# A two-layer Fourier and sliding-window attention kernel: zeros ahead of the first rows, and the last round's norm steps spread

## The chip, the cores and the metric

One core of a Trainium2 chip runs the whole program in one launch. The metric is device time in microseconds: 2034.66 is the median of three runs (2031.99, 2034.66, 2038.42). Five engines each work through a queue of their own: PE (TensorE, matrix products), DVE (VectorE), ACT (ScalarE), POOL (GpSimd) and SP (SyncE, which here issues nearly every DMA). In the profile PEld is the loading of weights into TensorE.

## The reference

The input x has 2048 rows and 640 columns. Two layers of different kinds follow each other, twice:

```python
x = x + _A_ref(_layernorm(x), dft_seq_re, dft_seq_im, dft_hid_re, dft_hid_im)   # spectral
x = x + _B_ref(_layernorm(x), wqkv, wo)                                         # attention
x = x + _A_ref(...)
x = x + _B_ref(...)

# A: a = x @ hid_re.T ; b = x @ hid_im.T ; y = seq_re @ a - seq_im @ b
# B: qkv = x @ wqkv, 32 heads of 20; row q sees keys q-255..q; softmax; @ wo
```

All data is float32. The layer norm subtracts a row's mean and divides by sqrt(variance + 1e-5).

## The kernel before, in words

**Precision.** TensorE multiplies float16. Each float32 operand is therefore kept as two float16 parts, a high part (a rounded copy) and a low part (what is left), and each product is three matrix products: high by high, high by low, low by high. Making the parts is much of what ACT (high parts), DVE (low parts) and POOL do.

**A spectral layer.** `spectral` first multiplies the normed rows with the hidden-size matrices (`z_stage`) and then with the sequence matrix, in four rounds r of eight steps j. For each step a 1 MB piece of the matrix is loaded by SP (`load_c`, tile `cq`), POOL makes four sums of its quarters (`take_c`, L549 to L552, tile `cs`), and seven high parts (ACT, L557) and seven low parts (DVE, L560) of quarters and sums become `cc`. The step's seven products use them, each of twelve 128x320 matmuls (`main_a`, `main_b`, `main_c`, banks x, y, z). Results are added into `res` by DVE (`add`, L583), ACT (L602) and POOL (L603, L613, L624).

After each product stands one `tick()`. A tick issues one of the splits of a coming piece, and one step of each generator in the list `side`. So work beside the products is placed by how many `yield`s stand between its instructions: a yield is one product, about 1.6 us of TensorE.

In the last round (r=3) the finished rows x2 are stored, and attention's input is begun there. `finish(0, ..)` and `finish(1, ..)`, chained in `side` from the end of step j=0 on, load back two pages of 128 rows each and run `norm_steps` for the pair: statistics (L138, L141), the reciprocal root of the variance by three Newton steps on single columns (L147 to L155), then ACT's normed page `lny` (L163). `pace` is the number of ticks for each step of it. Then `transposed` (L449) turns a page: TensorE transposes it in float32 against an identity `idf`, three 128-column pieces and then two, into one of two PSUM banks of tag f (`pf`), ACT makes the high part (L455), DVE the low part (L456, which frees the bank). As soon as `finish(0, ..)` is through, `ahead(proj)` issues ten query and key projections of 15 matmuls 128x256 each. Their evacuation is ACT `qf` (L386), POOL's cast (L387) and subtraction (L388), and a store to `qkd`; from there SP loads the stacks `ks` for the scores, behind tiles of ones.

**An attention layer.** `attention` interleaves scores, softmax and values, in a fixed order of TensorE, with units of other work from a list `fill`: value projections (the first of which stands right behind the last product of the spectral layer), query and key projections, output tiles ("out"), and, in layer 0 alone, the next layer's first hidden products ("next", from `Hidden.stage` with once=True). `next_unit` takes the unit due first out of those that are ready, in wide slots and narrow ones. L1272 is ACT's exponential, whose table ACT loads at L1411 before the first one.

**What sets the order.** The kernel writes the order by hand: each engine issues in the order in which the program states, with some instructions held behind others. At the start of layer 0 the order of loads on SP's queue, and DVE's splits of the first matrix pieces (L560) and of the first rows (L456), come from the lines of `spectral` around `constants()`, `load_c(0)` and `take_c(0)`.

Of the kernel before, what the change touches and what calls it, by code (L numbers as in the profile page):

```python
# [13 lines left out]
I32 = mybir.dt.int32  # L14
AF = mybir.ActivationFunctionType
# [58 lines left out]
def body(ctx: ExitStack, tc: tile.TileContext, x_in, cmat, whid, wqkv, wo, out):  # L74
# [56 lines left out]
    def norm_steps(xs, ys, act=False):  # L131

        n = len(xs)
        mv = keep.tile([P, n, 2], F32, tag=f"lnmv{n}", name="lnmv", bufs=2)
        for k, x in enumerate(xs):
            st = keep.tile([P, 2, 6], F32, tag="lnst", name="lnst", bufs=2)
            for h in range(2):
                nc.vector.bn_stats(st[:, h], x[:, h * 320:(h + 1) * 320])  # L138
                if h == 0:
                    yield  # L140
            nc.vector.bn_aggr(mv[:, k], st.rearrange("p a b -> p (a b)"))  # L141
            yield
        t = keep.tile([P, 3, n], F32, tag=f"lnt{n}", name="lnt", bufs=2)
        ts = nc.vector.tensor_scalar
        for k in range(n):
            h, g, u = (t[:, m, k:k + 1] for m in range(3))
            ts(h, mv[:, k, 1:2], 1e-5, -0.5 * X_UP ** -2, op0=OP.add, op1=OP.mult)  # L147
            ts(g.bitcast(I32), h.bitcast(I32), -0.5, ROOT, op0=OP.mult, op1=OP.add)
            for m in range(3):
                ts(u, g, g, h, op0=OP.mult, op1=OP.mult)  # L150
                normed[0] = ts(g, u, 1.5, g, op0=OP.add, op1=OP.mult).ins  # L151
                if m == 0:
                    yield
            if act:
                normed[0] = ts(u, mv[:, k, 0:1], g, -1.0, op0=OP.mult, op1=OP.mult).ins  # L155
            yield
        for _ in range(2 if act else 0):
            yield
        for k, x in enumerate(xs):
            g, u = t[:, 1, k:k + 1], t[:, 2, k:k + 1]  # L160
            y = keep.tile([P, D], F32, tag="lny", name="lny", bufs=2)
            if act:
                nc.scalar.activation(y, x, AF.Identity, bias=u, scale=g)  # L163
            else:
                normed[0] = ts(y, x, mv[:, k, 0:1], g, op0=OP.subtract, op1=OP.mult).ins
            ys.append(y)
            yield
# [55 lines left out]
    class Hidden:  # L223
# [29 lines left out]
        def stage(self, s, pool, new=new_f, once=False):  # L253
# [21 lines left out]
                z = z[:, :HD]  # L275

            def parts(m, f):
                nc.scalar.activation(zc[:, m, 0], f, AF.Copy)  # L278
                nc.gpsimd.tensor_tensor(zc[:, m, 1], f, zc[:, m, 0], op=OP.subtract)  # L279

            def scaled(o):
# [118 lines left out]
    def spectral(layer, res_src, hidden, first):  # L400
        with ExitStack() as st:
# [226 lines left out]
            def main_c(r, j):  # L628
                res, cc, y, zb = state.pop((r, j))
                x0, x1 = res  # L630
                z = product(r, zb, cc, 6, False, True)
                add(x0[:, hi], z, x0[:, hi])
                tick()
                z = product(r, y, cc, 5, False, True)
                add(x1[:, lo], z, x1[:, lo])
                last = r == NR - 1
                for k in range(2):
                    load((x2_d if last else acc_d)[2 * j + k], res[k])
                if last and j == 0:
                    side.append(chain(finish(0, 1), finish(1, 1)))  # L640
                tick()

            def ahead(proj):
                while finished[0] < 2:
                    yield 1
                yield 1
                for w in (1, 0):
                    for ct in range(ND):
                        for _ in proj.qk(0, w, ct):
                            pass  # L650
                        yield 1
# [98 lines left out]
                return [max(NJ * r + STAGES[r][k] - 3, k) for r in range(NR - 1)]  # L750

            if first:
                constants()
                x = [load_x(s) for s in range(2)]
                f = [load_w(n) for n in range(NXIN - 2)]
                norm_x(0, x[:1], nc.vector)
                for n in range(10):
                    split_w(n, f[n])
                    if n == 1:
                        turn_x(0)  # L760
                        turned_x(0)
                        norm_x(1, x[1:], nc.gpsimd)
                    if n == 7:
                        x = [load_x(s) for s in range(2, 4)]
                    if n + NXIN - 2 < 10:
                        f.append(load_w(n + NXIN - 2))
            load_c(0)
            for r in range(NR):
                for k in range(RS if r == 0 else 0):
                    s = RS * r + k  # L770
# [7 lines left out]
                            turn_x(s + 1, 2)  # L778
                    elif s > 1:
                        hidden.fetch(s)  # L780
                    if r == 0 and k == 1:
                        load_c(1)
                        with behind() as order:
                            if not first:
                                order.enter_context(tc.issue_after(hidden.after))
                            take_c(0)
# [56 lines left out]
    def attention(layer, proj, dst, final):  # L843
        with ExitStack() as st:
# [261 lines left out]
            def next_unit(wide=None):  # L1106
# [3 lines left out]
                if 2 * left() >= must_to() - now[0] % (2 * NP):  # L1110
                    us = [u for u in us if must(u)] or us
                us = [u for u in us if u.wide == wide] or us
                u = min(us, key=lambda u: u.due)
                fill.remove(u)
                return u
# [396 lines left out]
```

## Time and profile before

| | us |
|---|---|
| median of three runs | 2034.66 |
| the profiled execution | 2034.73 |
| its span, first to last instruction | 2033.0 |
| PE busy | 1978.8 (97%) |
| DVE busy | 1556.2 (77%) |
| POOL busy | 1438.2 (71%) |
| ACT busy | 1098.1 (54%) |
| granted TensorE clock, mean | 0.999 |

A row of the timeline holds start, duration, engine, line of the code, operation, out<-in with partitions, shape and type, and the count of instructions. In brackets stands how long the engine was idle ahead of it, and what ended that. A row of windows holds the window, its length, the busy time of PE, PEld, DVE, ACT and POOL (with the count of instructions), the granted TensorE clock, the busy share of the DMA engines, and GB/s. A row of groups holds the busy time and the mean in ns of one instruction, and then the idle time before them with what ended it. Layer 0's last round ends near 548 us and layer 1's near 1554; attention 0 ends near 1010.

### The profile page before, as it was taken

How to read it: one execution, taken by the hardware profiler on the slowest of the kernel's cores; microseconds unless marked ns; L12 is line 12 of the kernel's file. 1: busy time of each engine (PE TensorE's matmuls, PEld its weight loads, DVE VectorE, ACT ScalarE, POOL GpSimd, SP SyncE). 2: the span in 40 equal slices, each digit the busy share in tenths (PEclk: the TensorE clock that was granted, in tenths of full speed). 3: DMA queues.
4: the chain of work that ended last, by engine and by line, in shares of the span. 5: the costliest groups of instructions: out<-in, count | busy, mean ns of one | idle time of the engine just before them, and what ended most of it. 6: DMA issues, size and time to landing. Idle time of an engine off the chain costs nothing.

```text
span 2033.0 us, 55567 instructions
## 1 busy us (share of the span) xinstructions
PE 1978.8 (97%) x21761; PEld 1446.6 (71%) x21761; DVE 1556.2 (77%) x3281; ACT 1098.1 (54%) x1962; POOL 1438.2 (71%) x2148
## 2 busy tenths in 40 slices
PE   7999999999999999999999999999999999999998
PEld 5777777776777777777667777777677677777765
DVE  8888788767688888777648778787766788886674
ACT  5444555543257677666644444444332577766665
POOL 4667788877568788765557778777774687777754
PEclk9999999999999999999999999999999999999999
DMA  8566467566545545434545465454754455443232
GB/s 276 185 195 212 167 212 233 184 240 213 144 99 130 126 112 122 101 100 114 157 133 179 157 183 183 150 171 150 266 184 122 106 124 123 118 120 94 75 81 80
DMA packets 280507, 311.08 MB, mean 153 GB/s; under 512 B 107572, under 2 KB 214836, under 8 KB 271156
## 3 DMA queue, kind: packets, MB, share of 16 engines
q1 hardware_dynamic: 279668, 306.88, 51.3%
q8 instruction: 170, 2.79, 0.6%
q14 instruction: 93, 0.76, 0.1%
q10 hardware_dynamic: 576, 0.66, 0.1%
HBM read 201.72 MB, written 83.46 MB: 140 GB/s over the span
## 4 chain that ended last, share of the span: by engine, by line
PE 72%; DVE 12%; issue 4%; ACT 3%; DMA 2%; POOL 2%; SPq 0%; DVEq 0%; ACTq 0%; POOLq 0%
PE pf L125 33%; PE y L125 12%; PE x L125 12%; PE z L125 8%; PE sk L125 5%; DVE cc L560 3%; PE sq L125 3%; DVE sq L1216 2%; ACT ptq L1272 2%; DVE m L1218 2%; DMA res<-accd 1%; DVE lnst L138 1%; DVE lnt L150 1%; DVE res L583 1%; DVE lnt L151 1%
## 5 line engine op out<-in xcount | busy, mean ns | idle before, releaser
L125 PEld LDWEIGHTS <-cc 128*128 128x128 f16 x5376 | 525.9, 98 | 211.2 <-issue 11.1
L1272 ACT ACTIVATE ptq<-sk,shift,alpha 128x768 f32<-128x768 f32 (+2 forms) x512 | 472.7, 945 | 134.2 <-PE sk L125 70.5
L125 PEld LDWEIGHTS <-big 128*128 128x128 f16 x4320 | 411.9, 98 | 132.9 <-issue 27.0
L1218 DVE TENSOR_REDUCE m<-sq 128x2 f32<-128x512 f32 (+1 forms) x512 | 345.2, 674 | 18.9
L557 ACT ACTIVATE cc<-cs 128x512 f16<-128x512 f32 x256 | 153.1, 623 | 273.0 <-POOL cs L550 151.5
L125 PE MATMUL pf<-early,big 128*128 128x256 f16 x2400 | 288.1, 273 | 4.2 <-ACT qf L386 3.8
L1216 DVE COPY_PREDICATED sq<-mask,sk 128x256 f32<-128x256 int32 x512 | 216.4, 423 | 69.3 <-PE sq L125 65.9
L125 PE MATMUL y<-zc,cc 128*128 128x320 f16 x1728 | 262.1, 299 | 3.2 <-DVE pf L583 3.2
L1276 POOL TENSOR_SCALAR_AFFINE_SELECT ptq<-ptq 128x512 f32<-128x512 f32 x224 | 142.7, 637 | 170.6 <-ACT ptq L1272 169.2
L560 DVE SCALAR_TENSOR_TENSOR cc<-cs,cc 128x512 f16<-128x512 f32 x256 | 246.4, 971 | 6.0 <-ACT cc L557 6.0
L560 DVE SCALAR_TENSOR_TENSOR cc<-cq,cc 128x512 f16<-128x512 f32 x192 | 204.4, 1066 | 0.1
L125 PE MATMUL pf<-ptq,v 128*32 128x128 f32 (+1 forms) x3840 | 183.9, 330 | 4.8 <-DVE x L990 3.7
L125 PE MATMUL z<-zc,cc 128*128 128x320 f16 x1152 | 177.7, 299 | 2.9 <-DVE res L583 1.9
L1278 POOL TENSOR_SCALAR_AFFINE_SELECT ptq<-ptq 128x512 f32<-128x512 f32 x256 | 164.6, 643 | 22.4 <-ACT ptq L1272 22.3
L125 PE MATMUL x<-zc,cc 128*128 128x320 f16 x1152 | 177.7, 299 | 0.0
L549 POOL TENSOR_TENSOR cs<-cq 128x512 f32<-128x512 f32 x64 | 85.3, 1333 | 87.8 <-DVE cc L560 64.8
L386 ACT ACTIVATE qf<-pf 128x256 f32<-128x256 f32 x160 | 60.9, 382 | 156.4 <-PE pf L125 108.4
L125 PEld LDWEIGHTS pf<-ptq,v 128*32 128x32 f32 x3840 | 110.9, 110 | 47.5 <-DVE x L990 5.7
L125 PE MATMUL pf<-big,early 128*128 128x320 f16 x960 | 141.4, 300 | 0.0
L125 PEld LDWEIGHTS <-qs 62*128 62x128 f16 x2688 | 90.2, 94 | 59.2 <-issue 56.0
L279 POOL TENSOR_TENSOR zc<-big,zc 128x320 f16<-128x320 f32 x96 | 74.7, 792 | 73.6 <-ACT zc L278 73.6
L125 PE MATMUL pf<-bo,ot 128*128 128x320 f16 x840 | 124.6, 301 | 0.8 <-DVE x L990 0.8
(147 smaller groups left out, 3443.3 us busy)
## 6 DMA issues: line engine op xcount, KB each, us to landing
cq<-in_cmat_dram SPq DMA_DIRECT2D x64, 1024.0 KB
accd<-res SPq DMA_DIRECT2D x96, 320.0 KB
res<-accd SPq DMA_DIRECT2D x96, 320.0 KB
x<-x2d SPq DMA_DIRECT2D x64, 320.0 KB
qkd<-early SPq DMA_DIRECT2D x160, 128.0 KB
ks<-qkd SPq DMA_DIRECT2D x108, 160.0 KB
qs<-qkd SPq DMA_DIRECT2D x84, 160.0 KB
x2d<-res SPq DMA_DIRECT2D x32, 320.0 KB
```

The source lines that it names most:

```text
L125: i = getattr(nc.tensor, what)(*args, **kw)
L138: nc.vector.bn_stats(st[:, h], x[:, h * 320:(h + 1) * 320])
L279: nc.gpsimd.tensor_tensor(zc[:, m, 1], f, zc[:, m, 0], op=OP.subtract)
L386: nc.scalar.activation(f, pf[:, :QB], AF.Copy, scale=down)
L549: g.tensor_tensor(s1, a21, a22, op=OP.add)
L557: nc.scalar.activation(cc[m][:, 0], f, AF.Copy, scale=C_UP)
L560: nc.vector.scalar_tensor_tensor(cc[m][:, 1], f, C_UP, cc[m][:, 0], op0=OP.mult, op1=OP.subtract)
L1216: marks["dve"] = nc.vector.copy_predicated(near[pi][:, :, 0], mask[:, None, :].to_broadcast([P, 2, P]), farq[pi]).ins
L1218: marks["dve"] = nc.vector.tensor_reduce(TOP[n][:, pi, :, k], near[pi][:, :, :1 + (i >= 1)], axis=AX.XY, op=OP.max).ins
L1272: marks["act"] = nc.scalar.activation(o[:, pi], tps[pi][:, :, first:], AF.Sigmoid, bias=shift, scale=alpha[:, 0:1]).ins
L1276: nc.gpsimd.affine_select(out=q[:, :, a0], in_=q[:, :, a0], pattern=[[0, 4], [-1, P]], base=0, channel_multiplier=1, compare_op=OP.is_gt, ...
L1278: ins = nc.gpsimd.affine_select(out=q[:, :, a0 + 2], in_=q[:, :, a0 + 2], pattern=[[0, 4], [1, P]], base=0, channel_multiplier=-1, compare ...
```

## The change

Five things change. (1) In the first layer, ahead of everything, DVE sets a tile to zero and TensorE does 28 matmuls 128x512 on it, whose result nobody reads. The statement `load_c(0)` stands later in the first layer, at s=1, and `load_c(1)` with `take_c(0)` one s later. (2) The eight copies that make a high part in the next layer's first hidden products (`parts`, once=True) go from ACT to POOL. (3) The Newton steps of a pair of pages run on both columns at once, with one tick after each of the three. (4) `finish(0, ..)` has pace 2 in the place of 1, and `ahead` waits one tick more. (5) `next_unit` prefers, where there is a choice, "next" units in narrow slots and others in wide ones.

```diff
@@ norm_steps
-        for k in range(n):
+        if n > 1 and act:
+            h, g, u = (t[:, m] for m in range(3))
+            ts(h, mv[:, :, 1], 1e-5, -0.5 * X_UP ** -2, op0=OP.add, op1=OP.mult)
+            ts(g.bitcast(I32), h.bitcast(I32), -0.5, ROOT, op0=OP.mult, op1=OP.add)
+            for m in range(3):
+                nc.vector.tensor_tensor(u, g, g, op=OP.mult)
+                nc.vector.tensor_tensor(u, u, h, op=OP.mult)
+                normed[0] = nc.vector.scalar_tensor_tensor(g, u, 1.5, g, op0=OP.add, op1=OP.mult).ins
+                yield
+            normed[0] = nc.vector.scalar_tensor_tensor(u, mv[:, :, 0], -1.0, g, op0=OP.mult, op1=OP.mult).ins
+            yield
+        for k in range(0 if n > 1 and act else n):
@@ Hidden.stage, parts
-                nc.scalar.activation(zc[:, m, 0], f, AF.Copy)
+                if once:
+                    nc.gpsimd.tensor_copy(zc[:, m, 0], f)
+                else:
+                    nc.scalar.activation(zc[:, m, 0], f, AF.Copy)
@@ main_c
-                    side.append(chain(finish(0, 1), finish(1, 1)))
+                    side.append(chain(finish(0, 2), finish(1, 1)))
@@ ahead
-                yield 1
+                for _ in range(2):
+                    yield 1
@@ spectral
             if first:
+                nc.vector.memset(bo[0][:, 0], 0.0)
+                pt = new_f()
+                for _ in range(28):
+                    matmul(pt, bo[0][:, 0, :P], bo[0][:, 0, :512], start=True, stop=True)
                 constants()
...
-            load_c(0)
+            if not first:
+                load_c(0)
...
-                    if r == 0 and k == 1:
+                    if first and r == 0 and k == 1:
+                        load_c(0)
+                    if r == 0 and k == 1 + first:
                         load_c(1)
@@ next_unit
                 us = [u for u in us if u.wide == wide] or us
+                us = [u for u in us if (u.kind == "next") != wide] or us
```

The order in which the instructions stand moves at three places. The first is DVE near the end of the first rows' work in layer 0 (`big` is the turned rows, `cc<-cq` a low part of the first matrix piece). Before:

```order
L285 SCALAR_TENSOR_TENSOR early<-y,early 128x320
L560 SCALAR_TENSOR_TENSOR cc<-cq,cc 128x512
L456 SCALAR_TENSOR_TENSOR big<-pf,big 128x384
L285 SCALAR_TENSOR_TENSOR early<-z,early 128x320
L285 SCALAR_TENSOR_TENSOR big<-z,big 128x320
L560 SCALAR_TENSOR_TENSOR cc<-cs,cc 128x512
L456 SCALAR_TENSOR_TENSOR big<-pf,big 128x256
```

The same place of the change (L560 is now L574, L456 is L470, L285 is L299):

```order
L299 SCALAR_TENSOR_TENSOR early<-y,early 128x320
L470 SCALAR_TENSOR_TENSOR big<-pf,big 128x384
L299 SCALAR_TENSOR_TENSOR early<-z,early 128x320
L299 SCALAR_TENSOR_TENSOR big<-z,big 128x320
L470 SCALAR_TENSOR_TENSOR big<-pf,big 128x256
L574 SCALAR_TENSOR_TENSOR cc<-cq,cc 128x512 x3
```

The rows' low parts stand ahead of the piece's low parts, and no longer among them. On SP, the loads of the first piece stand at the same place as before.

The second place is the norm of a pair of pages on DVE in the last round, from the second aggregate on. Before:

```order
L141 BN_AGGR lnmv<-lnst 128x2
L148 TENSOR_SCALAR lnt<-lnt 128x1
L560 SCALAR_TENSOR_TENSOR cc<-cq,cc 128x512
L150 TENSOR_SCALAR lnt<-lnt 128x1
L147 TENSOR_SCALAR lnt<-lnmv 128x1
L583 SCALAR_TENSOR_TENSOR res<-z,res 128x320
L151 TENSOR_SCALAR lnt<-lnt 128x1
L148 TENSOR_SCALAR lnt<-lnt 128x1
L560 SCALAR_TENSOR_TENSOR cc<-cs,cc 128x512
L150 TENSOR_SCALAR lnt<-lnt 128x1 x2
L151 TENSOR_SCALAR lnt<-lnt 128x1 x2
```

The change, from the first root instruction on (L583 is now L597):

```order
L147 TENSOR_SCALAR lnt<-lnmv 128x2
L574 SCALAR_TENSOR_TENSOR cc<-cs,cc 128x512
L148 TENSOR_SCALAR lnt<-lnt 128x2
L150 TENSOR_TENSOR lnt<-lnt 128x2
L151 TENSOR_TENSOR lnt<-lnt 128x2
L152 SCALAR_TENSOR_TENSOR lnt<-lnt 128x2
L597 SCALAR_TENSOR_TENSOR res<-z,res 128x320
L574 SCALAR_TENSOR_TENSOR cc<-cs,cc 128x512
L150 TENSOR_TENSOR lnt<-lnt 128x2
```

An instruction now does both columns of the pair, and adds (L597) stand between the three Newton steps.

The third place is ACT at the end of the last round of layer 0, with what each instruction waits for (`early` is the turned pages, `lny` the normed ones, L1411 the exponential's table and its first use). Before:

```order
L455 ACTIVATE early<-pf 128x384 [waits PE_49]
L455 ACTIVATE early<-pf 128x256 [waits PE_49]
L602 ACTIVATE pf<-x 128x320 [waits PE_49,Pool_49]
L557 ACTIVATE cc<-cs 128x512
L1411 ACT_TABLE_LOAD [waits PE_49,Activation_49]
L1411 ACTIVATE first<-shift 128x1 [waits Pool_49]
L902 ACTIVATE v<-pf 128x16x20 [waits PE_49] x2
```

The change (L163 is now L174, L455 is L469, L1411 is L1434, L902 is L924):

```order
L571 ACTIVATE cc<-cs 128x512
L174 ACTIVATE lny<-x_6339,lnt 128x640 [waits DMAHW0_49,DVE_49]
L174 ACTIVATE lny<-x_6340,lnt 128x640 [waits DMAHW3_49]
L1434 ACT_TABLE_LOAD [waits PE_49,Activation_49]
L1434 ACTIVATE first<-shift 128x1 [waits Pool_49]
L469 ACTIVATE early<-pf 128x384 [waits PE_49]
L469 ACTIVATE early<-pf 128x256 [waits PE_49]
L924 ACTIVATE v<-pf 128x16x20 [waits PE_49] x2
```

The second pair's normed pages and their evacuations have moved behind all splits of the spectral layer, the evacuations behind the table load too, directly ahead of the first value projection. On TensorE the ten transposes of that pair stand there in a row:

```order
L125 MATMUL pf<-idf,lny 128x128 [waits Activation_49]
L125 MATMUL pf<-idf,lny 128x128 x4
L125 MATMUL pf<-idf,lny 128x128 [waits DVE_49]
L125 MATMUL pf<-idf,lny 128x128 x2
L125 MATMUL pf<-idf,lny 128x128 [waits DVE_49]
L125 MATMUL pf<-idf,lny 128x128
L125 LDWEIGHTS early
L125 MATMUL pf<-big,early 128x320 [waits DVE_49]
```

Before, they stand in four groups between the products of step j=7, and nothing stands between the last product and the projection.

## The prediction

> **What bounds the kernel now.** I read the page's busy shares and the chain of waits first, then the timeline at each place that the change touches, then windows and groups there.
>
> ```profile
> PE 1978.8 (97%) x21761; PEld 1446.6 (71%) x21761; DVE 1556.2 (77%) x3281; ACT 1098.1 (54%) x1962; POOL 1438.2 (71%) x2148
> ...
> PE 72%; DVE 12%; issue 4%; ACT 3%; DMA 2%; POOL 2%; SPq 0%; DVEq 0%; ACTq 0%; POOLq 0%
> ...
> 250.00:300.00 50.00, 50.00 (x372) 36.23 (x370) 40.28 (x68) 27.76 (x55) 42.26 (x35) 1.00 0.62 209
> ```
>
> TensorE is busy 1978.8 of a span of 2033.0 us, and in the middle of a spectral layer 50.00 of 50.00 at granted clock 1.00. So an edit can only win part of the 54.2 us in which TensorE stands still, or of the time at a lower clock, and it loses whatever new standstill it makes. No matmul that the result needs is removed. The profiled execution took 2034.73 us, 1.73 around its span; the median of the runs is 2034.66, so a sum made on the one holds for the other.
>
> **Start: zeros, and the order behind them.** These rows are the first work.
>
> ```profile
> 3.88 0.89 DVE L138 BATCH_NORM_STATS2 lnst<-xin 128x6 f32<-128x320 f32 x2 [3.88 <-DMA xin<-in_x_dram]
> 8.47 1.30 PE L125 MATMUL pf<-idf,lny 128*128 128x128 f32 x5 [8.47 <-DVE lny L165]
> 9.38 0.81 ACT L455 ACTIVATE big<-pf 128x384 f16<-128x384 f32 x2
> 9.93 0.72 PE L125 MATMUL y<-big 128*128 128x320 f16 x2 [0.15 <-ACT big L455]
> 10.76 0.88 DVE L456 SCALAR_TENSOR_TENSOR big<-pf,big 128x384 f16<-128x384 f32 x2
> 12.58 1.11 PE L125 MATMUL z<-big 128*128 128x320 f16 x7
> ```
>
> The memset is on DVE, idle until 3.88; it costs nothing. The first two 320-column products start .50 apart (9.93 to the next row at 10.43), so about .25 each; seven later take about .95, .135 each. Scaled to 512 columns, 28 zero products last 28 x .40 = 11.2 us if all run at the slow rate, 6.0 if all at the fast. With the slow rate for the first 3 to 4 us I estimate 7 to 8 us; starting near 1.2 us, they end at 8.1 to 9.2, beside a first need for TensorE at 8.47. ACT finishes its high parts at 10.19, DVE starts the low parts at 10.76: .57 of slack. Nor does a faster TensorE here gain: it then waits for DVE (2.13 us of work in the three between 14 and 17). I take **0**, between -0.3 and +0.75, and +3.9 if all 28 run slow (1.2 + 11.2 = 12.4 against 8.47).
>
> ```profile
> 14.00:17.00 3.00, 2.13 (x16) 1.41 (x15) 3.00 (x3) 0.91 (x2) 2.92 (x2) 1.00 0.76 213
> 31.04 1.28 DVE L560 SCALAR_TENSOR_TENSOR cc<-cq,cc 128x512 f16<-128x512 f32 x2
> 33.04 0.68 DVE L560 SCALAR_TENSOR_TENSOR cc<-cq,cc 128x512 f16<-128x512 f32 x1
> 34.25 1.40 PE L125 MATMUL x<-big 128*128 128x320 f16 x9 [1.52 <-DVE big L456]
> 41.79 0.55 DVE L456 SCALAR_TENSOR_TENSOR big<-pf,big 128x384 f16<-128x384 f32 x1
> ```
>
> In the program's order of the changed kernel, the first piece's four quarter loads stand where they stood in the SP queue, fourth behind the first rows, so that part **does not do what its words say**: nothing of the loads moves. What moves is DVE: L456 now stands ahead of three low parts of the matrix (1.28 + .68 us) instead of behind them. The 1.52 us wait at 34.25 can go; but the next L456, at 41.79, has the same DVE work ahead of it, less some .5 to 1.0 that the row order saves, so TensorE catches up with DVE there. I take **-0.8**, from -1.6 (the wait, wholly) to +0.3 (the split of a piece that comes later).
>
> **Last round of each spectral layer: norm steps spread.** Between the products of step j=6, DVE has the norm's small instructions ahead of the adds that TensorE waits for.
>
> ```profile
> 466.93 1.79 PE L125 MATMUL z<-zc,cc 128*128 128x320 f16 x12 [1.05 <-DVE res L583]
> 470.32 3.42 PE L125 MATMUL y<-zc,cc 128*128 128x320 f16 x24 [1.59 <-DVE pf L583]
> 494.39 1.80 PE L125 MATMUL pf<-early,big 128*128 128x256 f16 x15 [1.47 <-ACT qf L386]
> 1472.85 1.79 PE L125 MATMUL z<-zc,cc 128*128 128x320 f16 x12 [1.04 <-ACT cc L557]
> 1476.23 3.42 PE L125 MATMUL y<-zc,cc 128*128 128x320 f16 x24 [1.59 <-DVE pf L583]
> 1500.29 1.80 PE L125 MATMUL pf<-early,big 128*128 128x256 f16 x15 [1.46 <-ACT qf L386]
> ...
> 468.25 0.44 DVE L150 TENSOR_SCALAR lnt<-lnt 128x1 f32<-128x1 f32 x2
> 469.78 0.48 DVE L583 SCALAR_TENSOR_TENSOR pf<-y,pf 128x320 f32<-128x320 f32 x1
> ```
>
> The six waits sum to 1.05 + 1.59 + 1.47 + 1.04 + 1.59 + 1.46 = 8.2 us. The roots of two pages were 18 instructions a pair; ten of them fill the block from 468.25 to the add at 469.78, .15 us each. Together they are 12, and no more than five stand between two adds. An instruction on 128x2 is not in the trace; it lies between the .15 of 128x1 and the .48 of 128x320, and I take .2. So a pair costs 2.4 us instead of 2.7, but in portions of 1 us and less with an add between them. Low parts of the matrix that DVE owes at that time (.68 each alone, as at 33.04) are still there, so I leave .8 of each layer's wait standing, and .3 for a query/key evacuation: 8.2 - 2 x 1.1, **-6.0**, from -8.2 to -3.
>
> **What is pushed back.** The same spread delays all that follows. Before, the ten transposes of pages 2 and 3 stand between j=7's products, their evacuations hidden under 1.6 us products:
>
> ```profile
> 530.30 0.49 PE L125 MATMUL pf<-idf,lny 128*128 128x128 f32 x3
> 530.63 1.79 PE L125 MATMUL y<-zc,cc 128*128 128x320 f16 x12
> 532.26 0.38 PE L125 MATMUL pf<-idf,lny 128*128 128x128 f32 x2
> 535.22 0.48 ACT L455 ACTIVATE early<-pf 128x384 f16<-128x384 f32 x1
> 535.74 0.56 DVE L456 SCALAR_TENSOR_TENSOR early<-pf,early 128x384 f16<-128x384 f32 x1 [0.85 <-ACT early L455]
> 536.48 0.38 ACT L455 ACTIVATE early<-pf 128x256 f16<-128x256 f32 x1 [0.78 <-PE pf L125]
> ...
> 547.69 2.20 PE L125 MATMUL pf<-big,early 128*128 128x320 f16 x15
> 547.96 1.28 ACT L1411 ACT_TABLE_LOAD   x1 [11.09 <-PE y L125]
> 1553.88 0.20 ACT L1411 ACTIVATE first<-shift 128x1 f32<-128x1 f32 x1 [11.11 <-PE y L125]
> ```
>
> After, all ten stand in a row behind the last product and ahead of the first value projection (547.69 here), through two PSUM buffers, and ACT's table load with `first` stands ahead of their evacuations. In layer 0, from the end of the products at E0: table load and `first` to about 1.75; ACT .48 to 2.25; DVE .56 to 2.8, which frees the first buffer; transposes .33 (530.30 to 530.63) and two thirds of it, .22, another ACT .48 and .38, DVE .56 and the rest of its start delays: the projection starts at about E0 + 4.6. Among the products the ten took 2 x (.33 + .22) = 1.1 of TensorE anyway, so +3.5. Layer 1 has no table load in its row, which saves about 1.2: E0 + 3.4, +2.3. Sum **+5.8**; from +3 (the order within the row overlaps better) to +8.
>
> A stall of that length may also cost clock:
>
> ```profile
> 1000.13 0.31 PE L125 MATMUL sk<-ks,qs 62*128 62x128 f16 x4 [1.81 <-ACT ptq L1272]
> ...
> 999.00:1002.00 3.00, 1.77 (x37) 1.28 (x40) 2.85 (x7) 2.18 (x4) 1.81 (x4) 0.96 0.00 0
> 1002.00:1005.00 3.00, 3.00 (x33) 1.63 (x25) 1.53 (x3) 1.21 (x2) 1.82 (x5) 0.50 0.84 250
> ```
>
> After 1.81 us of standstill the three us from 1002 were granted .50: about 1.6 us of work lost. I take one such window, **+1.7**, in one of the layers, between 0 and two (+3.4).
>
> [...]
>
> **Tail of attention 0.** Eight of ACT's copies become POOL casts.
>
> ```profile
> L278 ACT ACTIVATE early<-big 128x320 f16<-128x320 f32 x8 | 3.7, 466 | 3.7 <-DVE big L288 3.7
> L298 POOL CAST early<-big 128x320 f16<-128x320 f32 x6 | 3.4, 574 | 0.0
> L125 PE MATMUL sk<-ks,qs 62*128 62x128 f16 x64 | 4.6, 219 | 2.9 <-ACT ptq L1272 2.9
> ```
>
> ACT loses 8 x .466 = 3.7 us, POOL gains 8 x .574 = 4.6, at a place where ACT's exponentials (L1272) are what TensorE waits for (2.9 us from 945 to 1002, 1.81 of them in the stall above, 1.1 in small waits). The filter on units exchanges one 15-product unit between a wide and a narrow slot. I take half of it: .9 of the 1.81, .8 of the half clock behind it, .5 of the small waits, **-2.2**; from -4.5 (all of them) to +2 (POOL's 4.6 us land ahead of its masks, which the next products need).
>
> **Sum:** 0 - 0.8 - 6.0 + 5.8 + 1.7 - 2.2 = -1.5, so 2034.7 - 1.5 = **2033.2 us**.
>
> **Rivals.** *The debt goes and nothing else comes* (faster): waits go whole (-8.2), the clock does not halve, the tail's stall goes (-4.0), the start gives -0.8, against +5.8: -7.2, about 2027.5. For it: the six waits are plain in the rows, and 1.81 us sets the clock back only in one place. Against: DVE is busy all of the five us there.
>
> ```profile
> 465.00:470.00 5.00, 2.67 (x19) 1.66 (x18) 5.00 (x21) 2.68 (x6) 2.78 (x3) 1.00 0.57 198
> ...
> 529.02 6.55 SPq L187 DMA_DIRECT2D ks<-qkd  x6
> 537.17 6.31 SPq L187 DMA_DIRECT2D ks<-qkd  x6
> ```
>
> *The first keys come late* (slower): the spread moves the last query/key projections from among j=6 and j=7 to just ahead of j=7, and the twelve loads of the K and Q stacks behind them. Ten of these remain to be issued after the last store, 1.07 us each (6.4/6), 10.7 us; with the store's and the load's way, some 3 each by estimate, they are in at about 17 us after the last projection, and the first scores need them after nine products of 1.63, the stall of 4.6 and a projection of 2.0: 21.3 us. It decides only from 1.5 us a load; at 2 it costs 4 us a layer and gives 2041.5. Against: the rows measure 1.07.
>
> [...]
>
> **Numbers.** This kernel's measurement can tell about 0.3%, 6.1 us. Forecast .56, its own range 2029 to 2039; first rival .27; late keys .09; both clocks .08. Faster by over 0.3% (under 2028.6): most of the first rival and a little of the forecast's low end, .28. Slower (over 2040.8): the late keys, and .05 from the forecast's and the clock's upper ends, .14. Same: .58. The range reaches from 2026 into the first rival to 2040.5, where the late keys begin.
>
> **What would show it.** Right: the waits of over a us at j=6 gone in both layers; TensorE idle about 3.5 and 2.3 us around ten transposes just ahead of the first value projection, with ACT's table load first in layer 0; a granted clock near .5 behind one of them; the zeros ending at 8 to 9 us; a smaller stall near 1000 us. Wrong: transposes that overlap in those stalls (then it is faster), a first score matmul released by a load of the stacks, or zeros that reach past 9.5 us.

## The result, and the profile after

The changed kernel takes 2041.55 us (median of 7 runs, 2039.42 to 2044.26), the kernel before 2034.91 beside it: a ratio of 1.0036, 95% interval 1.0026 to 1.0046. It is slower by 0.36%, and it lies 1 us above the upper end of the predicted range (2040.5). The profiled execution has a span of 2040.2 us against 2033.0. One run of the experiments below, of the kernel with single columns at pace 2, took 2526.53 us at a granted clock of 0.752, and the median given there, 2039.57, is that of its seven other runs (2040.32 with it).

Where the 7.2 us came from can be read off by setting the same TensorE work of both traces beside each other. The start of the first sequence product, of the first value projection of each attention layer, and so on, are milestones; the table holds how far the change moves each stage between them. A turn is the passage from one round of eight steps into the next.

| stage | predicted, us | measured, us |
|---|---|---|
| start, to the first sequence product | -0.8 | -1.86 (48.42 against 50.28) |
| waits for DVE and ACT in the last rounds, layer 0 and 1 | -6.0 | +1.84 and +1.85; at layer 0's turn into that round +.78 more, at layer 1's -.35 |
| ten transposes in a row, layer 0 | +3.5 | +3.75 |
| ten transposes in a row, layer 1 | +2.3 | +2.29 |
| half clock behind such a row | +1.7 | +2.24, in layer 0 alone |
| attention of layer 0 | -2.2 | -3.4 |
| all else | 0 | 0.0 |
| sum | -1.5 | +7.2 |

The first fence shows the timeline of TensorE in the changed kernel: the start, the last round of layer 0 with its waits, one row of layer 1, and the rows of ten transposes with the projections behind them.

```profile
1.30 7.66 PE L125 MATMUL pf<-bo 128*128 128x512 f16 x28 [1.30 <-DVE bo L768]
8.80 0.71 PE L125 MATMUL pf<-idf,lny 128*128 128x128 f32 x5
48.42 0.98 PE L125 MATMUL x<-early,cc 128*128 128x320 f16 x6
...
466.02 1.79 PE L125 MATMUL z<-zc,cc 128*128 128x320 f16 x12 [1.18 <-DVE res L597]
476.07 1.79 PE L125 MATMUL y<-zc,cc 128*128 128x320 f16 x12 [1.66 <-DVE pf L597]
480.54 1.79 PE L125 MATMUL z<-zc,cc 128*128 128x320 f16 x12 [1.05 <-DVE res L597]
502.87 0.55 PE L125 MATMUL pf<-idf,lny 128*128 128x128 f32 x3 [2.06 <-DVE early L470]
547.55 0.71 PE L125 MATMUL pf<-idf,lny 128*128 128x128 f32 x5
550.34 1.31 PE L125 MATMUL pf<-idf,lny 128*128 128x128 f32 x5 [2.08 <-DVE early L470]
552.39 4.16 PE L125 MATMUL pf<-big,early 128*128 128x320 f16 x15 [0.74 <-DVE early L470]
...
1513.02 0.55 PE L125 MATMUL pf<-idf,lny 128*128 128x128 f32 x3 [2.05 <-DVE early L470]
1557.71 0.71 PE L125 MATMUL pf<-idf,lny 128*128 128x128 f32 x5
1559.37 0.77 PE L125 MATMUL pf<-idf,lny 128*128 128x128 f32 x5 [0.95 <-DVE early L470]
1561.09 2.20 PE L125 MATMUL pf<-big,early 128*128 128x320 f16 x15 [0.94 <-DVE early L470]
```

Layer 0's waits are now 1.18 + 1.66 + 1.05 + 2.06 = 5.95 us, where there were 4.11. From the first transposes of the row to the projection pass 552.39 - 547.55 = 4.84 us in layer 0 and 1561.09 - 1557.71 = 3.38 in layer 1; less the 1.09 that the ten cost before, that is +3.75 and +2.29. In layer 0 the projection's 15 products take 4.16 us instead of 2.20, and the second five transposes ahead of it take 1.31 us where layer 1's take .77. The granted clock says why (windows of the same kernel, the last of layer 1):

```profile
548.00:552.00 4.00, 1.57 (x8) 1.06 (x7) 1.90 (x6) 2.70 (x6) 0.75 (x16) 0.80 0.91 328
552.00:556.00 4.00, 3.61 (x14) 2.01 (x14) 0.67 (x2) 0.07 (x1) 0.00 (x0) 0.50 0.11 42
556.00:560.00 4.00, 4.00 (x35) 2.30 (x33) 2.04 (x5) 0.87 (x2) 0.00 (x0) 0.85 0.00 0
1560.00:1564.00 4.00, 3.06 (x26) 1.89 (x24) 1.32 (x3) 1.16 (x3) 0.00 (x0) 1.00 0.84 312
```

The waits at the two turns are not the norm's: the kernels with the start alone and with the zeros alone, described below, have .80 and .86 us at layer 0's turn without any edit of the last round.

What made the norm's waits longer is on DVE and POOL. The next rows are the timeline of those two engines in step j=6 of layer 0; L150 to L152 are the two-column root instructions.

```profile
470.11 0.16 DVE L152 SCALAR_TENSOR_TENSOR lnt<-lnt 128x2 f32<-128x2 f32 x1
471.35 1.26 POOL L563 TENSOR_TENSOR cs<-cq 128x512 f32<-128x512 f32 x1 [2.36 <-DVE lnt L150]
471.38 1.26 DVE L151 TENSOR_TENSOR lnt<-lnt 128x2 f32<-128x2 f32 x1
472.57 1.27 POOL L565 TENSOR_TENSOR cs<-cq 128x512 f32<-128x512 f32 x1
472.67 1.19 DVE L152 SCALAR_TENSOR_TENSOR lnt<-lnt 128x2 f32<-128x2 f32 x1
473.78 0.48 DVE L597 SCALAR_TENSOR_TENSOR res<-y,res 128x320 f32<-128x320 f32 x1
474.18 1.43 DVE L574 SCALAR_TENSOR_TENSOR cc<-cq,cc 128x512 f16<-128x512 f32 x1
475.54 0.48 DVE L597 SCALAR_TENSOR_TENSOR pf<-y,pf 128x320 f32<-128x320 f32 x1
```

An instruction on two columns takes .16 us while POOL stands still (at 470.11, inside POOL's 2.36 us of idleness), and 1.26 and 1.19 where a POOL sum runs: the two end at 472.64 and 473.86, the sums at 472.61 and 473.84. The add at 475.54 stands behind these and behind a low part of 1.43 us, and TensorE waits 1.66 us for it.

The fourth wait, 2.06 us in layer 0, has ACT behind it (timeline of TensorE, POOL, ACT and DVE):

```profile
498.43 1.72 POOL L564 TENSOR_TENSOR cs<-cs,cq 128x512 f32<-128x512 f32 x1
498.79 0.38 PE L125 MATMUL pf<-idf,lny 128*128 128x128 f32 x2
500.18 1.15 ACT L571 ACTIVATE cc<-cs 128x512 f16<-128x512 f32 x2 [2.73 <-POOL cs L564]
501.23 0.61 ACT L571 ACTIVATE cc<-cq 128x512 f16<-128x512 f32 x1
501.75 0.74 ACT L469 ACTIVATE early<-pf 128x384 f16<-128x384 f32 x2
502.25 0.56 DVE L470 SCALAR_TENSOR_TENSOR early<-pf,early 128x384 f16<-128x384 f32 x1 [3.24 <-ACT early L469]
```

The first page's transposes end at 499.17. Their evacuation (L469) stands in ACT's queue behind high parts of the next piece, and these wait for POOL's sums: ACT is idle for 2.73 us, until the sum of L564 ends at 500.15, and comes to the evacuation at 501.75. DVE stands idle for 3.24 us, and TensorE cannot turn the second page until a bank is free.

### The profile page after: what moved, and what is told of

It is laid out like the page before. It is cut to its first block, busy times and chain, and to the rows that moved or that the text cites. A ratio compares the mean times of both kernels' runs of the same rounds, so it can differ in the third digit from the quotient of the medians.

```text
span 2040.2 us, 55608 instructions
## 1 busy us (share of the span) xinstructions
PE 1986.6 (97%) x21789; PEld 1447.3 (71%) x21789; DVE 1565.0 (77%) x3258; ACT 1096.1 (54%) x1954; POOL 1444.5 (71%) x2156
## 4 chain that ended last, share of the span: by engine, by line
PE 69%; DVE 14%; issue 4%; DMA 3%; ACT 3%; POOL 3%; SPq 1%; DVEq 0%; ACTq 0%; POOLq 0%
PE pf L125 32%; PE y L125 11%; PE x L125 11%; PE z L125 7%; PE sk L125 5%; DVE cc L574 3%; PE sq L125 3%; DVE sq L1239 2%; DMA res<-accd 2%; DVE m L1241 2%; ACT ptq L1295 2%; DVE res L597 1%; DVE lnst L138 1%; DVE lnt L161 1%; DVE x L1012 1%
## 5 line engine op out<-in xcount | busy, mean ns | idle before, releaser
L574 DVE SCALAR_TENSOR_TENSOR cc<-cs,cc 128x512 f16<-128x512 f32 x256 | 247.5, 976 | 5.0 <-ACT cc L571 5.0
L574 DVE SCALAR_TENSOR_TENSOR cc<-cq,cc 128x512 f16<-128x512 f32 x192 | 211.2, 1102 | 0.1
```

What stands on the lines that cost most here:

```text
L574: nc.vector.scalar_tensor_tensor(cc[m][:, 1], f, C_UP, cc[m][:, 0], op0=OP.mult, op1=OP.subtract)
```

## The experiments

**The pace.** In the changed kernel, pace 1 and one tick again; everything else stays.

```diff
-                    side.append(chain(finish(0, 2), finish(1, 1)))
+                    side.append(chain(finish(0, 1), finish(1, 1)))
...
-                for _ in range(2):
-                    yield 1
+                yield 1
```

> The changed kernel with pace 1 and one tick again (the two-column roots, the start and the tail stay). Theory A, that the spread's cost is the row of ten transposes ahead of the first value projection, the half clock behind it in layer 0 and the 2.06 us wait of the third transposes: the row goes back among the products, the projection follows the last product without a gap in both layers, TensorE's clock stays full there, and the time falls from 2041.5 by 3.75 + 2.29 + 2.2 = 8.2, or 9.4 if the transposes' wait of 2.06 falls to the 1.47 of before: 2032 to 2033.5. Theory B, that the two-column roots are what costs and the spread only moved things: the time stays above 2037.

Measured: 2027.32 us, a ratio of 0.9962 (0.9947 to 0.9977) to the kernel before, 14 us below the changed one. Theory A has the direction and the transposes back among the products, but it falls short by some 5 us. Timeline of TensorE:

```profile
467.70 1.79 PE L125 MATMUL z<-zc,cc 128*128 128x320 f16 x12 [1.53 <-ACT cc L571]
480.74 0.55 PE L125 MATMUL pf<-idf,lny 128*128 128x128 f32 x3 [0.93 <-DVE early L470]
546.09 2.20 PE L125 MATMUL pf<-big,early 128*128 128x320 f16 x15
```

The waits of the round are 1.53 + .93 = 2.46 us, against 5.95 at pace 2 and 4.11 before the change. Layer 1 has 1.52 + .91 against 5.94. So the spread's cost has three parts: the row of transposes (3.75 + 2.29), the clock (2.2), and 3.5 us of waits in each layer, of which the expectation held .6 at most. They make 15.3; the first sequence product of this execution comes 1.0 later (49.43), which leaves the 14.3 that the spans differ by.

**The columns.** In the changed kernel each two-column instruction is two single-column ones, with the other factor as a per-row scalar; same ticks, same order.

```diff
-            for m in range(3):
-                nc.vector.tensor_tensor(u, g, g, op=OP.mult)
-                nc.vector.tensor_tensor(u, u, h, op=OP.mult)
-                normed[0] = nc.vector.scalar_tensor_tensor(g, u, 1.5, g, op0=OP.add, op1=OP.mult).ins
-                yield
+            for m in range(3):
+                for h, g, u in cols:
+                    ts(u, g, g, h, op0=OP.mult, op1=OP.mult)
+                    normed[0] = ts(g, u, 1.5, g, op0=OP.add, op1=OP.mult).ins
+                yield
```

> The changed kernel, in which each two-column root instruction is two single-column ones (tensor_scalar, with the other factor as a per-row scalar), in the same places and with the same ticks: 18 instead of 12 a pair. Theory A, that the two-column forms wait for GpSimd (1.26, 1.19, .82, .81 and .79 us beside a GpSimd instruction that ends with them, .15 alone): each single-column one takes .1 to .27 and DVE gets some 2.5 us back in the first pair; the wait of 1.66 in each layer falls below .7 and the time by 2 to 4, to 2037.5 to 2039.5. Theory B, that DVE's debt is the low parts of the matrix alone: the waits of 1.66 and 1.05 stay within .3 and the time within 1 of 2041.5.

Measured: 2039.57 us, ratio 1.0025 (1.0014 to 1.0035), 2.0 below the changed kernel by the medians; the intervals of the two ratios overlap. Groups of DVE in the last round of layer 0 (window 440 to 510), first of the changed kernel:

```profile
L151 DVE TENSOR_TENSOR lnt<-lnt 128x2 f32<-128x2 f32 x3 | 2.2, 734 | 0.1
L152 DVE SCALAR_TENSOR_TENSOR lnt<-lnt 128x2 f32<-128x2 f32 x3 | 1.5, 504 | 0.1
L150 DVE TENSOR_TENSOR lnt<-lnt 128x2 f32<-128x2 f32 x3 | 1.1, 375 | 0.0
```

and of the one with single columns:

```profile
L152 DVE TENSOR_SCALAR lnt<-lnt 128x1 f32<-128x1 f32 x6 | 1.3, 264 | 0.0
L153 DVE TENSOR_SCALAR lnt<-lnt 128x1 f32<-128x1 f32 x6 | 1.0, 204 | 0.0
```

Nine two-column instructions took 4.8 us, the twelve single-column ones that do the same take 2.3. That POOL does not hold the single-column ones up is seen where a sum of 1.27 us runs beside them, and two take .45 and two .33 (timeline of DVE and POOL, single columns):

```profile
471.24 0.45 DVE L152 TENSOR_SCALAR lnt<-lnt 128x1 f32<-128x1 f32 x2
471.40 1.27 POOL L565 TENSOR_TENSOR cs<-cq 128x512 f32<-128x512 f32 x1 [2.43 <-DVE cc L576]
471.61 0.33 DVE L153 TENSOR_SCALAR lnt<-lnt 128x1 f32<-128x1 f32 x2
```

The waits on the roots shrink as theory A has it: 1.66 and 1.05 become one of .28. By the medians the time follows by 2.0 us, at the edge of what theory A expected, and the timeline shows where the gain went:

```profile
479.56 3.42 PE L125 MATMUL y<-zc,cc 128*128 128x320 f16 x24 [0.28 <-DVE pf L599]
501.08 0.55 PE L125 MATMUL pf<-idf,lny 128*128 128x128 f32 x3 [2.89 <-DVE early L472]
...
500.00:504.00 4.00, 2.92 (x14) 1.89 (x15) 3.53 (x7) 1.20 (x4) 2.26 (x3) 0.73 0.00 0
1508.00:1512.00 4.00, 4.00 (x21) 2.67 (x20) 4.00 (x8) 0.87 (x2) 3.13 (x3) 0.59 0.02 4
```

The wait for the transposes' evacuation grows from 2.06 to 2.89 us in layer 0 and from 2.05 to 2.85 in layer 1, and the granted clock falls behind it in both. What DVE won earlier is waited for later, at ACT's queue. The row of ten transposes in layer 0 runs at full clock in this execution and takes 4.50 us, with the same stall of 2.08 us in it.

**Both edits of the last round undone.** Zeros, load order, copies and filter stay.

```diff
-        if n > 1 and act:
...
-        for k in range(0 if n > 1 and act else n):
+        for k in range(n):
...
-                    side.append(chain(finish(0, 2), finish(1, 1)))
+                    side.append(chain(finish(0, 1), finish(1, 1)))
```

> The changed kernel without both edits of the last round (roots, pace and tick as before); zeros, load order, GpSimd copies and the units' filter stay. If the stages add up as the two profiles read (start -1.9, attention of layer 0 -3.4, the end -.3, the last rounds +6.9 and +4.1 with the clock): 2034.9 - 5.6 = 2029.3, faster than both. If the gain of the attention layer came from the other arrival time of its first values rather than from the copies and the filter: about 2033.

Measured: 2029.1 us, ratio 0.997 (0.9959 to 0.9981), as the stages' sum has it. So the last round's edits are the whole of the loss, and the rest of the change gains some 6 us (3.9 to 8.3 by the interval).

**Single columns at pace 1.** The edits of the first two experiments together.

```diff
-                nc.vector.tensor_tensor(u, g, g, op=OP.mult)
+                for h, g, u in cols:
+                    ts(u, g, g, h, op0=OP.mult, op1=OP.mult)
...
-                    side.append(chain(finish(0, 2), finish(1, 1)))
+                    side.append(chain(finish(0, 1), finish(1, 1)))
```

> The changed kernel with pace 1 and one tick as before, and single-column roots with a tick after each Newton step. Against the same kernel with two-column roots, which took 2027.3: if the two-column forms' waits for GpSimd reach TensorE at pace 1 too, DVE gets 2 to 3 us a layer back and the time falls by 1 to 2, to 2025.3 to 2026.3. If at pace 1 GpSimd is idle beside most of them (it waits for DVE there) and TensorE's waits come from the low parts: 2026.5 to 2028. [...]

Measured: 2028.01 us, ratio 0.9964 (0.995 to 0.9978). With this there are four kernels that differ in pace and columns alone (pace 1 has one tick ahead of the projections, pace 2 has two; the next experiment tells what that tick costs):

| | pace 1 | pace 2 |
|---|---|---|
| two columns | 2027.3 | 2041.6 |
| single columns, three ticks | 2028.0 | 2039.6 |

The pace costs 12 to 14 us either way. Two columns in the place of single ones move the time by -0.7 at pace 1 and +2.0 at pace 2, which these runs do not tell from nothing; the expected 1 to 2 us do not come. In the traces the waits over .7 us at pace 1, from the statistics on, are 2.46 and 2.43 us in the two layers with two columns, and 3.40 and 3.50 with single ones: there TensorE does not wait longer for the two-column form.

**The tick ahead of the projections.** Pace 1, but the second tick stays.

```diff
-                    side.append(chain(finish(0, 2), finish(1, 1)))
+                    side.append(chain(finish(0, 1), finish(1, 1)))
```

> The changed kernel with pace 1 for the first pair; the second tick ahead of the query and key projections stays. If the pace alone is what moved the transposes and the late waits, it comes out like the kernel without both, 2027.3 within 1. If the later projections cost something by themselves: 2029 or more.

Measured: 2027.67 us, ratio 0.9962 (0.9949 to 0.9975). The tick costs nothing; it is the pace.

**Work in the row's stall.** In the changed kernel eleven 128x512 products in the row of ten transposes of layer 0.

```diff
                         transposed(y, m, proj.rows[j][0][:, k])
+                        if first and j == 1 and m == 1:
+                            pt = new_bank("x")
+                            for _ in range(3 if k else 8):
+                                matmul(pt, bo[0][:, 0, :P], bo[0][:, 0, :512], start=True, stop=True)
```

> The changed kernel with eleven more 128x512 products, whose results nobody reads, inside the row of ten transposes of layer 0: eight where TensorE stood for 2.08 us, three where it stood for .74. If it is the standing still there that halves the clock (4.16 us for the projection's 15 products in place of 2.20, and the rows behind it), the granted clock stays 1.00 and the time falls by about 2, to 2039.5. If the half clock there is a matter of chance in the one profiled execution, or is set by something else: no change in the median, 2041.5 or up to .5 more.

Measured: 2041.8 us, ratio 1.0028 (1.0018 to 1.0038): no change in the median. Its profiled execution:

```profile
549.82 0.71 PE L125 MATMUL pf<-idf,lny 128*128 128x128 f32 x5
550.37 1.89 PE L125 MATMUL x<-bo 128*128 128x512 f16 x8
552.61 0.77 PE L125 MATMUL pf<-idf,lny 128*128 128x128 f32 x5 [0.35 <-DVE early L470]
554.33 2.20 PE L125 MATMUL pf<-big,early 128*128 128x320 f16 x15 [0.30 <-DVE early L470]
...
500.00:504.00 4.00, 1.94 (x14) 1.31 (x12) 1.15 (x3) 2.32 (x5) 2.83 (x3) 0.95 0.31 86
504.00:508.00 4.00, 4.00 (x21) 2.53 (x19) 3.56 (x7) 0.87 (x2) 3.36 (x3) 0.62 0.00 0
```

Here the projection behind the row runs at full speed, but the clock is lost at 504, behind the 2.06 us wait for the transposes of the first pair, which is the same as in the changed kernel and cost no clock there. So one profile is too little to say where the clock goes. The means over whole executions say more: the changed kernel was granted below 1.000 in six of seven, the kernel with this filling in nine of ten, the one with both edits of the last round undone in none of seven. An execution of the changed kernel at 1.000 has a span of 2037.7, one at .997 of 2042.5. That the filling saves the clock at the row is not shown: the kernel with single columns kept it there without any filling.

**The start alone.** The kernel before with zeros and later load statements.

```diff
+                nc.vector.memset(bo[0][:, 0], 0.0)
+                pt = new_f()
+                for _ in range(28):
+                    matmul(pt, bo[0][:, 0, :P], bo[0][:, 0, :512], start=True, stop=True)
...
-            load_c(0)
+            if not first:
+                load_c(0)
```

> The kernel before with the zeros and the later load statement alone. If the 1.86 us won by the first sequence product last to the end: 2033.0. If DVE takes them back at the turn to the last round (a wait of .78 that is new there): 2033.8. If the start gives nothing at the end: 2034.9.

Measured: 2031.6 us, ratio 0.9981 (0.9971 to 0.9991), which is 1.8 to 5.9 us below the kernel before: the gain stays to the end. That it is more than the expected 1.9 is not shown.

**Zeros alone, and the order alone**, each in the kernel before. First the zeros:

```diff
+                nc.vector.memset(bo[0][:, 0], 0.0)
+                pt = new_f()
+                for _ in range(28):
+                    matmul(pt, bo[0][:, 0, :P], bo[0][:, 0, :512], start=True, stop=True)
```

> The kernel before with the 28 zero products and nothing else. The zeros end at 8.8 to 10.1 us in the runs so far, the first product follows them by 1.1. If the whole gain of the start (1.2 to 1.9) is that the rows' low parts stand ahead of the matrix's: the first sequence product comes at 50.3 or up to .7 later, 2034.9 to 2035.5. If the faster first products count: at 49.3, and 2033.8.

Then the order:

```diff
-            load_c(0)
+            if not first:
+                load_c(0)
...
-                    if r == 0 and k == 1:
+                    if first and r == 0 and k == 1:
+                        load_c(0)
+                    if r == 0 and k == 1 + first:
```

> The kernel before with the later load statements and no zeros. The zeros alone put the first sequence product at 51.31 (50.28 before), the two together at 49.11. If the two add up, the order alone puts it at 48.1, and the time is 2034.9 - 2.2 = 2032.7. If the order gains only because the zeros have raised the clock: 50.3 and 2034.9.

Measured: zeros 2033.64 us, ratio 0.9991 (0.9981 to 1.0); order 2033.29 us, ratio 0.9987 (0.9978 to 0.9996). In the profiled executions the first sequence product starts at 51.31 with the zeros alone, which is later by 1.0 than before, and with the order alone at

```profile
48.57 0.98 PE L125 MATMUL x<-early,cc 128*128 128x320 f16 x6
```

which is 1.7 earlier, with no zeros in the kernel. The start's gain is the order of DVE's work; the zeros give nothing that their own trace shows, and end after the first transposes could have begun (8.87 to 10.26 us in the nine kernels that have them, against 8.47). For the zeros neither expectation came: the first sequence product is later than the first of them had it, and the time is at the second's. Their interval reaches from 0 to 3.9 us gained, and their profile lacks the half clock at 1002 us that the kernel before has. Between 1.7 and the 2.2 of the expectation these times do not tell.

**The tail of attention 0.** The copies alone, the filter alone, and both.

```diff
-                nc.scalar.activation(zc[:, m, 0], f, AF.Copy)
+                if once:
+                    nc.gpsimd.tensor_copy(zc[:, m, 0], f)
+                else:
+                    nc.scalar.activation(zc[:, m, 0], f, AF.Copy)
```

```diff
                 us = [u for u in us if u.wide == wide] or us
+                us = [u for u in us if (u.kind == "next") != wide] or us
```

> The kernel before with the eight copies of the next layer's first products on GpSimd and nothing else. If ACT's relief ends the 1.81 us stall at 1000 us with its half clock: 2034.9 - 3.4 = 2031.5 and a granted clock of 1.00 behind it. If the choice of units does it: 2034.9, the stall of 1.8 stands.

> The kernel before with the units' filter and nothing else. If the choice of units gives the attention layer's gain: 2031.5, no half clock near 1000 us. If the copies do it: 2034.9 within 1.

> The kernel before with the copies on GpSimd and the units' filter together; each alone gave 2033.9. If they only work together, as in the changed kernel, whose attention layer is 3.2 shorter from the first wait of its tail to the next layer's first product: 2031.5. If they add up as single edits do: 2033.

Measured: copies 2033.85 us, ratio 0.9995 (0.9985 to 1.0004); filter 2033.96 us, 0.9999 (0.9989 to 1.0008); both 2032.75 us, 0.9989 (0.998 to 0.9998). Neither alone can be told from no change; the two together just can (0.4 to 4.1 us gained). The stall at 1000 us, in the timeline of TensorE of the three in this order:

```profile
1000.90 0.30 PE L125 MATMUL sk<-ks,qs 62*128 62x128 f16 x4 [1.83 <-ACT ptq L1275]
```

```profile
1002.33 0.30 PE L125 MATMUL sk<-ks,qs 62*128 62x128 f16 x4 [0.59 <-ACT ptq L1273]
```

```profile
999.11 0.31 PE L125 MATMUL sk<-ks,qs 62*128 62x128 f16 x4 [0.82 <-ACT ptq L1276]
```

ACT's relief does not shorten the stall; the order of the units does, and a longer wait for DVE takes its place further on (1.75 us at 1028 with both, 1.55 at 1032 with the filter alone, .65 there in the kernel before). So the expectation that the copies end the stall has fallen. That of the filter came for the stall, behind which its profile has no half clock, and not for the time.

## Why the prediction was wrong

**The step that failed** is the term of -6.0 us for the norm's waits, by about 10 us: the two layers' waits grew by 1.84 and 1.85. In layer 0 the wait at the statistics went from 1.05 to 1.18 and those on the roots from 1.59 to 2.71. The query and key evacuation's 1.47, of which the term left .3 standing, did go, and the transposes' 2.06 came in its place. Three parts of the term were wrong.

First, the price of a two-column instruction. The prediction put it between .15 and .48 us by size, and took .2. Size was not what set it. Twelve of them took 6.0 us in the first pair, not 2.4, since five of them ran beside a POOL instruction and ended with it, after .79 to 1.26 us. The rows of before that it had used showed single columns with a per-row scalar, which take .26 and .20 us beside a POOL add (at 466.16 and 466.80) and .27 and .20 where POOL stands still (at 469.59 and 469.47; .15 from one start to the next). This is shown by the rows and by the kernel with single columns, whose waits on the roots fall from 2.7 to .3. How much of the time hangs on it is not: the columns' form alone moved it by no more than these runs can tell.

Second, where the rest would go. The "low parts of the matrix that DVE owes" were left standing at .8 a layer; the first wait, which lies at the statistics ahead of the roots, was 1.05 before and is 1.18 after. Nothing in the change touches it, and it should have been left out of the gain. Single columns at pace 2 still have it, at 1.19.

Third, and largest, a stall that the prediction did not see: the first pair's transposes, delayed as the second pair's are, come to a place where ACT's queue holds high parts that wait for POOL. It costs 2.06 us in each layer, and 2.89 where DVE has been relieved. At pace 1 the same wait is .93. The prediction followed the delay of the second pair to the end of the round and did not ask the same of the first.

**What held.** The row of ten transposes: 4.6 and 3.4 us were worked out from the ACT, DVE and TensorE rows of before with two banks, and 4.84 and 3.38 measured. Of the difference between the layers, 1.46, the wait behind the table load is 1.13 (2.08 against .95). Transposes at half clock make .54, less .20 at the last wait. At full clock, in the kernel with single columns, layer 0's row takes 4.50 us. Pace 1 removes the rows, so their cause is shown. The half clock came behind one of the two rows, 2.24 against 1.7, but its place is luck: the kernel with single columns kept the clock at that row, behind the same stall, and lost it behind the first pair's transposes in both layers. Pace 1 removes these stalls together, so which of them costs the clock in the changed kernel's other executions stays open. The zeros end at 8.96 us in the profiled execution, inside 8.1 to 9.2, but past 9.5, the prediction's own sign of being wrong, in six of the eight other kernels that have them. Their weight loads are .43 us apart from 1.70 to 4.26 and nine take 1.83 from there on, so the slow rate, which the prediction put at 3 to 4 us by estimate, held for 3.0 from the first product at 1.30. First loads: the queue was unchanged, as the order had it.

**Too small or for another reason.** The start gave -1.86 instead of -0.8: the claim that TensorE catches up with DVE at the next L456 was wrong, since the order alone keeps its 1.7 us to the first sequence product. The zeros, put at no more than +.75, alone put that product 1.0 later. The tail gave -3.4 instead of -2.2, but in the place of the copies it is copies and unit order together; and some 1.6 us of it is a half clock in the profile of the kernel before, behind a stall of 1.81 us that cost no clock in the profiles with the zeros alone and with the order alone (1.82).

**The rivals.** Late keys did not come: no score matmul waits for the stacks in either layer. The 3 us that this rival put on a store's and on a load's way are near what the trace of before has: SP waits up to 3.9 us for a store to `qkd` (17 waits, 43.1 us), and the first load, issued at .79, is read at 3.88. Half clock at both rows, to which the prediction gave .08, did not come either: the granted clock is 1.00 in layer 1 (1560 to 1564). Slower was the right side, but with 2.2 us of clock and 3.7 of waits. Pace 1 with the rest of the change gives the first rival's figure (2027.3 against 2027.5), but by luck: that rival had all 8.2 us of waits go against 5.8 for the rows, and at pace 1 there are no rows and the waits fall by 3.3, from 8.2 to 4.9.

## What to carry to other kernels

Spreading small work over more ticks delays all that hangs on it. Follow each instruction to its new place and ask what stands ahead of it on every engine there, for the first block as well as the last: here a pace of 2 instead of 1 cost 12 to 14 us, most of it by moving transposes out of their cover. And the price of a small VectorE instruction was not its size here: one on two columns took .15 or .16 us alone and up to 1.26 beside a GpSimd instruction, with which it ended, and one with a per-row scalar on one column took .26 beside a GpSimd add of 1.31 (at 466.16 in the kernel before).

## What the runs showed that was not expected

In fourteen profiled executions, between 20 us and the closing stretch from 2024 us on, the clock was halved seven times, for 3.41 us in six of them and for twice that, 6.83, in one. It was halved only behind stalls of TensorE of 1.81 us or longer (1.81 to 2.89), and never where the longest stall was 1.75. The window of the kernel before from end to end of its half clock:

```profile
1001.79:1005.20 3.41, 3.41 (x34) 1.96 (x27) 1.72 (x3) 1.42 (x4) 1.82 (x5) 0.50 0.78 237
```

But such a stall does not always do it: the changed kernel's two waits for the first pair's transposes, 2.06 and 2.05 us, cost none in its profile. The stall of 1.81 to 1.83 us at 1000 cost the clock in the kernel before, in that with the copies and in that with the start alone, and cost none in that with the zeros or with the order alone. First the kernel with the start alone, then that with the zeros alone (windows behind the stall):

```profile
1000.00:1004.00 4.00, 4.00 (x40) 2.26 (x33) 1.98 (x4) 1.69 (x4) 1.82 (x5) 0.57 0.60 181
```

```profile
1002.00:1005.00 3.00, 3.00 (x48) 1.98 (x48) 2.56 (x5) 2.32 (x4) 1.49 (x3) 1.00 0.33 118
```

What decides between the two these runs do not show. Kernels without such a stall keep a mean of 1.000 in most executions (six kernels whose profile has no stall over 1.75 us: 36 of 41; of them the one with both edits of the last round undone in all seven), and between executions of the changed kernel the clock goes with spans 1 to 5 us longer.
